# Weights in fp32 pieces on SyncE cast by GpSimd, a later gate for batch 2, and identity matmuls ahead of the first transposes

## Chip, cores, metric

One core of a Trainium2 chip. The metric is the device time of one execution in microseconds (us), median of several. "Ratio" is always the mean time of one kernel's fast runs over the mean of the fast runs of the kernel before of the same rounds, with a 95% interval; so it is not quite the ratio of the medians quoted beside it. Single executions of one kernel spread by 1 to 2 us.

Names: PE is TensorE, PEld its weight loads, DVE VectorE, ACT ScalarE, POOL GpSimd, SP SyncE. L824 is a line of the kernel; lines differ between versions. The granted clock is the share of its full speed that PE was given, by the profile. The milestone, below, is the start of the transposes of batch 1's first head group.

## The reference

```python
q_s = softmax(q, axis=-1); k_s = softmax(k, axis=2)        # 8 batches, 8 heads, 576 x 64
x = q_s @ (k_s^T @ v)                                      # heads put side by side: (8, 576, 512)
x_prev = x shifted by one position
xk = mu_k * x + (1 - mu_k) * x_prev
xr = mu_r * x + (1 - mu_r) * x_prev
k = relu(xk @ w_k)                                         # 512 -> 1024
out = sigmoid(xr @ w_r) * ((k * k) @ w_v)                  # 1024 -> 512
```

(Cut: the maxima and 1e-9 of the softmax, which the kernel leaves out.)

## The kernel before

A small planner in the kernel gives every piece of work an engine, an estimated length and a key, simulates the engines and emits each engine's instructions in the order that it finds. Each engine then runs its list in order, so the list decides what waits behind what. The parts that the argument touches (cuts marked):

```python
# weights: DMA with a cast, issued by GpSimd, after the eighth of batch 0's twelve loads
def emit_wk(g, c, e):
    ap = bass.AP(tensor=moe_w_k.tensor, ...)
    dst = wks[g][:, c * 2 // F, :, :] if split[g] else wks[g][:]          # bf16
    return nc.gpsimd.dma_start(out=dst, in_=ap)
# ... wr and wv likewise

# k = relu(...)^2: ScalarE evacuates, VectorE squares: two inputs, both in SBUF
def relu():
    nc.scalar.activation(out=rels[...], in_=bank(kf)[:, 0:n], func=ACT.Relu, scale=HALF_ROOT)
def square():
    nc.vector.tensor_tensor(out=k2s[...], in0=rels[...], in1=rels[...], op=ALU.mult)

# mu, transposed on PE into one of the four rotating banks (mm_a..mm_d), copied by VectorE
def emit_mu():
    nc.tensor.transpose(out=bank(mu_slot)[:, 0:8], in_=mu_sb[:], identity=identf[:])
def emit_mu_copy():
    nc.vector.tensor_copy(out=mu[:], in_=bank(mu_slot)[:, 0:8])
# ...
for op in plan.order():
    op.made = op.emit()
```

Batches 0 and 1 are prepared in the start: transposes of q and kv = k^T v of one head group ("transposes and kv": 72 small matmuls and as many weight loads, 0.66 us together at full speed), then "mixing" (products of 288 columns with mu folded in), then 32 k matmuls of 512 columns, then the transposes and kv of batch 1's first head group.

The softmax here doesn't subtract the row's maximum and nothing guards it: scores larger than these inputs give would overflow.

## Time and profile before

| | us |
|---|---|
| median of 3 runs | 201.63 (201.58 to 202.44) |
| first k matmul on record | 18.30 |
| PE at full speed from | about 22 |
| all 32 k matmuls done | 27.96 |
| transposes of batch 1's first group | 28.92, with 4 r matmuls done ahead of them |

Most lines behind this are in the prediction; the last is this one of the timeline of PE:

```profile
28.92 0.48 PE L507 MATMUL att_b<-ident,qs_a 64*64 64x64 bf16 x36
```

The trace has 2147 matmul records for 2171 weight loads, so some 24 matmuls are missing from it, among them the very first k matmul, here and in every trace of this study but those of the last three runs. Its weight load stands at 17.88 here, and the "0.34 <-issue" ahead of the first k matmul on record is no wait.

PE is full from 25 us to the end, so only the start has room.

### The profile page before, as it was taken

What the parts mean: (1) busy time and instruction counts of PE and PEld (TensorE: products, weight loads), DVE (VectorE), ACT (ScalarE), POOL (GpSimd) and SP (SyncE); (2) the same over time, 40 slices, a digit from 0 to 9 for tenths busy, and PEclk for the clock granted to TensorE, in tenths of its full rate; (3) what the DMA queues carried; (4) which work ended last, traced back from release to release, by engine and by line L of the source; (5) the groups of instructions that cost most, each with busy time, mean ns of one, the idle gap of its engine ahead of it and who ended that gap; (6) DMA issues with size and microseconds to landing.
All of it is one profiled execution on the core that took longest, in us unless ns stands there. A gap on an engine that the chain in (4) does not pass through costs nothing.

```text
span 200.2 us, 5314 instructions
## 1 busy us (share of the span) xinstructions
PE 183.6 (92%) x2147; PEld 96.6 (48%) x2171; DVE 160.6 (80%) x348; ACT 136.9 (68%) x212; POOL 40.7 (20%) x66
## 2 busy tenths in 40 slices
PE   2547999999999999999999999999999999999992
PEld 0234554545444555454476455455455544544761
DVE  2498469798999999999979999999998998432531
ACT  5494595998999799978559978946842662552440
POOL 1584365644354123411300000000000000000000
PEclk9999999999999999999999999999999999999998
DMA  6999999999999999993991220242042204402514
GB/s 196 348 277 227 281 256 352 391 398 412 388 403 405 403 405 362 398 378 110 262 365 47 54 56 0 52 111 51 3 100 62 52 3 105 105 0 54 118 41 105
DMA packets 15520, 40.72 MB, mean 203 GB/s; under 512 B 2300, under 2 KB 3592, under 8 KB 15496
## 3 DMA queue, kind: packets, MB, share of 16 engines
q0 software_dynamic: 7840, 27.40, 40.6%
q1 hardware_dynamic: 7208, 12.26, 21.4%
q10 hardware_dynamic: 448, 0.72, 1.2%
q8 instruction: 17, 0.28, 0.6%
q14 instruction: 7, 0.06, 0.1%
HBM read 33.56 MB, written 9.44 MB: 215 GB/s over the span
## 4 chain that ended last, share of the span: by engine, by line
PE 88%; DMA 4%; DVE 3%; issue 1%; ACT 1%; DVEq 0%
PE mm_c L766 10%; PE mm_a L722 10%; PE mm_d L722 9%; PE mm_d L766 8%; PE mm_a L766 7%; PE mm_c L722 7%; PE mm_b L766 6%; PE mm_b L722 6%; PE mm_b L756 6%; PE mm_d L756 4%; PE mm_c L756 3%; PE att_b L520 3%; PE mm_a L756 3%; DMA raw_d<-in_q_dram 3%; PE att_a L520 3%; PE att_b L507 2%
## 5 line engine op out<-in xcount | busy, mean ns | idle before, releaser
L722 PEld LDWEIGHTS <-wk 128*128 128x128 bf16 x320 | 35.4, 114 | 27.7 <-issue 2.2
L722 PE MATMUL mm_a<-xk,wk 128*128 128x512 bf16 (+1 forms) x96 | 24.2, 362 | 0.3 <-issue 0.2
L722 PE MATMUL mm_d<-xk,wk 128*128 128x512 bf16 (+1 forms) x87 | 22.4, 370 | 0.1
L766 PEld LDWEIGHTS <-k_b 128*128 128x128 bf16 x152 | 14.5, 98 | 15.7 <-issue 0.7
L756 PEld LDWEIGHTS <-xr 128*128 128x128 bf16 x144 | 13.9, 98 | 15.9
L766 PEld LDWEIGHTS <-k_a 128*128 128x128 bf16 x144 | 13.4, 97 | 15.5 <-issue 0.4
L722 PE MATMUL mm_c<-xk,wk 128*128 128x512 bf16 (+1 forms) x66 | 16.0, 358 | 0.4 <-issue 0.3
L722 PE MATMUL mm_b<-xk,wk 128*128 128x512 bf16 (+1 forms) x62 | 15.5, 352 | 0.2
L756 PE MATMUL mm_b<-wr_bf,xr 128*128 128x512 bf16 x50 | 13.3, 379 | 0.1
L766 PE MATMUL mm_c<-wv_bf,k_a 128*128 128x512 bf16 x46 | 12.1, 379 | 0.2 <-issue 0.2
L766 PE MATMUL mm_c<-wv_bf,k_b 128*128 128x512 bf16 x47 | 12.1, 379 | 0.2 <-issue 0.2
L761 ACT ACTIVATE th_a<-mm_b 128x512 f32<-128x512 f32 x12 | 7.1, 595 | 6.4 <-PE mm_b L756 4.9
L766 PE MATMUL mm_d<-wv_bf,k_b 128*128 128x512 bf16 x39 | 10.1, 379 | 0.2 <-issue 0.2
L766 PE MATMUL mm_b<-wv_bf,k_a 128*128 128x512 bf16 x38 | 10.0, 379 | 0.2 <-issue 0.2
L766 PE MATMUL mm_a<-wv_bf,k_b 128*128 128x512 bf16 (+1 forms) x39 | 9.4, 358 | 0.1
L756 PE MATMUL mm_d<-wr_bf,xr 128*128 128x512 bf16 x34 | 9.1, 379 | 0.1
L766 PE MATMUL mm_d<-wv_bf,k_a 128*128 128x512 bf16 x28 | 7.5, 379 | 0.4 <-issue 0.3
L710 DVE TENSOR_TENSOR k_a<-rel_b 128x512 bf16<-128x512 bf16 (+1 forms) x14 | 5.6, 398 | 2.8 <-ACT rel_b L706 2.8
L710 DVE TENSOR_TENSOR k_a<-rel_c 128x512 bf16<-128x512 bf16 (+1 forms) x13 | 5.1, 389 | 3.4 <-ACT rel_c L706 3.4
L761 ACT ACTIVATE th_b<-mm_c 128x512 f32<-128x512 f32 x6 | 3.7, 610 | 5.6 <-PE mm_c L756 4.7
L756 PE MATMUL mm_c<-wr_bf,xr 128*128 128x512 bf16 x28 | 7.2, 379 | 0.1
L756 PE MATMUL mm_a<-wr_bf,xr 128*128 128x512 bf16 x28 | 7.2, 379 | 0.0
(275 smaller groups left out, 416.7 us busy)
## 6 DMA issues: line engine op xcount, KB each, us to landing
out_dram<-ot_a SPq DMA_DIRECT2D x24, 128.0 KB, 3.8
out_dram<-ot_b SPq DMA_DIRECT2D x24, 128.0 KB, 3.0
out_dram<-ot_c SPq DMA_DIRECT2D x22, 128.0 KB, 2.8
raw_b<-in_k_dram POOLq DMA_DIRECT2D x3, 576.0 KB, 9.4
raw_c<-in_v_dram POOLq DMA_DIRECT2D x3, 576.0 KB, 8.9
raw_d<-in_q_dram POOLq DMA_DIRECT2D x3, 576.0 KB, 10.1
raw_a<-in_q_dram POOLq DMA_DIRECT2D x2, 576.0 KB, 10.5
raw_e<-in_k_dram POOLq DMA_DIRECT2D x2, 576.0 KB, 11.6
```

The costliest lines, as they stand in the source:

```text
L507: nc.tensor.transpose(out=transposed()[64 * u:64 * u + 64, hf, 64 * j:64 * j + 64], in_=qss[qs.index][r, j, 64 * u:64 * u + 64], identity= ...
L520: nc.tensor.matmul(bank(xp)[64 * hf:64 * hf + 64, u, at + c:at + e], lhsT=w[r, hf, :], rhs=qts[qt.index][r, hf, src:src + e - c], start=(n ...
L710: nc.vector.tensor_tensor(out=k2s[k2.index][:, fc, 0:n], in0=rels[rel.index][:, 0:n], in1=rels[rel.index][:, 0:n], op=ALU.mult)
L722: nc.tensor.matmul(bank(kf)[:, 0:n], lhsT=(w[:, h, u, fc % 4:F // 2:4] if split[ct // 2] else w[:, u, F // 2 * h + fc % 4:F // 2 * (h + 1) ...
L756: nc.tensor.matmul(bank(rps), lhsT=xs[1][:, ct, c:c + 128], rhs=wr_bf[:, ct // 2 + 2 * (ct % 2), :], start=(ct == 0), stop=(ct == CT - 1))
L761: nc.scalar.activation(out=ths[th.index][:], in_=bank(rps), func=ACT.Tanh, scale=0.5)
L766: nc.tensor.matmul(bank(vps)[:, 0:w], lhsT=k2s[k2.index][:, ft, 128 * m:128 * m + 128], rhs=wv_bf[:, ft, e:e + w], start=(ft == 0), stop=( ...
```

## The change

Its intent: weights come on the plain DMA queue in ten fp32 pieces of 512 KB, each early enough, and GpSimd, freed of issuing them, casts each into bf16. Batch 2's loads wait for the second half of batch 1's last q so that they do not take bandwidth from the start. Identity matmuls keep PE busy from 1.4 us, in the hope that its first k matmuls then run at full speed (in the kernel before PE was slow until about 22 us). The planner's offsets were tuned anew. Core of the diff:

```diff
-FIRST = ((0, 0, ("ACT", "ACT")), (0, 1, ("SP", "SP")), (0, 2, ("SP", "SP")), ...
+FIRST = ((0, 0, ("ACT", "ACT")), (1, 0, ("SP", "SP")), (0, 1, ("SP", "SP")), ...
-LOADS = ("q10a", "wk0a", "wk0b", "wk1", "k10a", ...
+LOADS = ("wk11", "k10a", "v10b", "wk01", "q10a", "q10b", "wr0", "k10b", "wk00", "wk10", ...
+W_CAST = ("POOL", "POOL", ... ten times)
-GATE = 7
-FILL = 0
+GATE = "q11b"
+FILL = 60
+    def load_weights(name, dst, offset, ap):
+        slot = Slot("raw")
+        ...
+        o = plan.add("SP", ..., lambda: nc.sync.dma_start(out=flat(), in_=...), [], [slot], ...)
+        return plan.add(e, ..., lambda: copies[e](out=dst[0], in_=flat()), [o], [], [slot])
     for _ in range(FILL):
+        plan.add("PE", 0.216, 0.386, 2 * LATE, lambda slot=slot: filler(slot), ...)
... (cut: NUDGE, 73 tuned offsets; EARLY, LOOK, SPARE, PACE; CASTS, now with all of batch 0's v on POOL; POOL's emit_wk, emit_wr, emit_wv removed)
```

Of the 60 identity matmuls (128x512) 18 find a place: 15 ahead of the first transposes, 3 later.

## The prediction

> **What bounds the kernel now.** I read the page first, then the busy times by stage, then PE's instructions in the start.
>
> The page: busy shares, PE by slices, DMA rate by slices (5 us each).
>
> ```profile
> PE 183.6 (92%) x2147; PEld 96.6 (48%) x2171; DVE 160.6 (80%) x348; ACT 136.9 (68%) x212; POOL 40.7 (20%) x66
> ...
> PE   2547999999999999999999999999999999999992
> ...
> GB/s 196 348 277 227 281 256 352 391 398 412 388 403 405 403 405 362 398 378 110 262 365 47 54 56 0 52 111 51 3 100 62 52 3 105 105 0 54 118 41 105
> ```
>
> PE is full from slice 5 to the last, so only the first 20 to 25 us can hold much. Busy times by stage (window, its length, then busy us and instructions of each engine):
>
> ```profile
> 8.00:18.30 10.30, 5.23 (x163) 3.94 (x153) 7.76 (x21) 7.03 (x11) 7.74 (x13) 1.00 1.05 271
> 18.30:24.50 6.20, 6.15 (x54) 2.88 (x55) 3.24 (x8) 2.60 (x6) 2.17 (x4) 1.00 1.12 279
> 24.50:44.40 19.90, 19.64 (x292) 9.88 (x295) 16.26 (x36) 16.96 (x30) 11.00 (x17) 1.00 1.04 350
> 44.40:196.00 151.60, 149.54 (x1616) 78.74 (x1633) 129.06 (x272) 105.67 (x164) 17.77 (x25) 1.00 0.54 177
> ```
>
> The second line looks full (6.15 of 6.20) and is not well used. The timeline of PE there (start, length, operation, shapes, count):
>
> ```profile
> 18.30 0.63 PE L722 MATMUL mm_c<-xk,wk 128*128 128x512 bf16 x1 [0.34 <-issue]
> ...
> 20.20 0.69 PE L520 MATMUL att_b<-qt_a,wp_b 64*64 64x288 bf16 x12
> ...
> 22.14 0.44 PE L520 MATMUL att_b<-qt_b,wp_d 64*64 64x288 bf16 x8
> 22.41 0.42 PE L520 MATMUL att_a<-qt_b,wp_d 64*64 64x288 bf16 x12
> ...
> 23.43 0.38 PE L722 MATMUL mm_d<-xk,wk 128*128 128x512 bf16 x1
> ```
>
> The same 12 products take 0.69 us at 20.2 and 0.42 at 22.4; a 512-column matmul 0.63 at 18.3 and 0.38 at 23.4. PE ran slow until about 22, though the granted-clock column says 1.00. And GpSimd, which issued the weights, held them back (waits of 8 to 31 us: total, times, longest):
>
> ```profile
> POOL raw_i L310 <- DMA wk<-in_moe_w_k_dram: 2.6, 1, 2.6
> POOL wv_bf L422 <- DMA wr_bf<-in_moe_w_r_dram: 2.0, 1, 2.0
> POOL raw_h L310 <- DMA wk<-in_moe_w_k_dram: 1.9, 1, 1.9
> ```
>
> The last wk wait ends at 21.99, and the first matmuls on wk's second half start at 22.76.
>
> **An account of PE.** Warm 512-column matmuls follow each other at 0.216 us (the chain shows 4 in 0.86). The network needs 288 for k, 144 for r, 288 for v: 720 x 0.216 = 155.4 us. Transposes and kv of one head group take 0.66 us (28.82 to 29.49 in the timeline), 16 times: 10.6. One mixing block of 20 products takes 0.72 with its changes of tile size, 8 times: 5.8. The other 12 x blocks take an estimated 0.3: 3.6. Together 175.4. The last matmul ends near 196.0, so about 20.5 us are lost, and 4.2 us follow. Before 18.3 PE does 2.8 us of this work (two pairs of transposes and kv, two mixing blocks): 15.5 lost. From 18.3 to 24.5 it does 4.9 (16 k matmuls, two blocks): 1.3 lost. From 44.4 to 196.0 it has 148.6 us of work left in 151.6: 3 lost in 150. The change lives in the first two terms.
>
> [...]
> - [...]0.69 against 0.42 us, changing near 22.0 after PE had been busy since 18.3.
> - [...]From 12 to 30 us 248 GB/s landed, 4.46 MB. I count 2.1 MB of it as bf16 weights that were read as 4.2 MB, so (4.46 + 2.1) / 18 = 364 GB/s were read, against 403 to 405 for plain loads in slices 12 to 15. The cast transfers thus cost nearly their fp32 bytes; fp32 pieces save about 10%, not half.
> - [...]the same 128x576 cast took 665 ns on POOL, 671 on ACT, 746 on DVE.
>
> **The change, part by part.**
> 1. *Weights.* Five cast transfers (512 or 256 KB of bf16) become ten fp32 ones of 512 KB on SyncE, each with a cast of 128x1024 on POOL: 665 x 1024/576 = an estimated 1.2 us, ten of them 12 us. [...]each piece needs 1.3 us of DMA at 404 GB/s, so POOL keeps up. But every piece has 1.2 us added before PE may use it.
> 2. *Order.* SyncE now issues wk11, k of batch 1 (half), wk01, q, wr0, k (half), wk00, wk10, wr1, v, four wv, then q, v, k of the second head group. Batch 0's 3.54 MB are down by about 12.1 (the last is used at 12.52 without a DMA wait). At 404 GB/s wk01 is complete after 1.34 MB more, 15.4; wk00 after 3.28, 20.2; wk10 after 3.80, 21.5; v after 4.91, 24.3; wv after 7.0, 29.5; the last k after 8.8, 33.8. [...]wk00 usable at 22.4, wk10 at 23.8.
> 3. *Identity matmuls.* Fifteen precede the first transposes: cold 0.43 each, some warm, so about 5 to 6 us from 1.4. They end before qs_a is complete (7.49) and delay nothing. With three more later, PE should stay warm through the start[...].
> 4. *Attention of batch 0.* The second q comes before k and v, so v lands at 9.5 to 10 instead of 8 to 8.6. POOL casts both v: two of 0.67, two mu_all pieces of 0.69, two of 0.67, and the second kv ends near 14.3 (before 14.7). In after's program all four mixing blocks come before the first k matmul. Walking their eight products (0.35 warm), evacuations (ACT 0.64, DVE 0.75) and the DVE weights (1.1 for four) through two att buffers, I get 18.4 for the first k matmul. Before had 18.3, with two blocks still to do.
> 5. *From there.* Sixteen warm k matmuls: 18.4 + 3.45 = 21.9. Wait for wk00 to 22.4, eight: 24.1; wk10 is there; eight more: 25.85, and the mu transpose, 26.0. Before finished all 32 at 27.96: 2.0 us gained.
> 6. *Given back.* Batch 1's v lands at 25.3 and ACT casts it in two of 0.67, so kv waits to 26.6: about 0.4 lost. wv is ahead of PE, which reaches v near 31. The second head group's k lands at 34.8, its exps end at 36.2, when PE gets there.
> 7. *After 44.* The same 150 us of work with a reordered list; 51 switches between small and full tiles against 49. I count nothing.
>
> Sum: -2.0 + 0.4, and -0.2 for the better-filled start of unit 1: about -1.8 us, 199.8.
>
> **Rivals.**
> - *POOL's casts become the bound.* If DVE and POOL hinder each other, a cast may take 1.8 us; ten are 18 and wv is late by some 3 us. For it: DVE is 76 to 82% busy in these stages. Against: POOL's 665 ns at 8 us, though DVE was idle then. It would make 201 to 202.5.
> - *PE goes cold again* between 8 and 18, as its waits there are long. The 16 k matmuls then cost up to 1.7 us more, half hidden in the wait for wk00: 200.8 to 201.5.
> - *The start is won in full*: mixing ends sooner and DMA lands without lag, and the retuned order takes 1 to 2 us of the 3 lost after 44. 197.3 to 198.5. For it: so many tuned offsets. Against: wk00's bytes cannot come before 20.2.
> - *Hidden anyway*: batch 2's loads, now gated on the second group's q (31 us), arrive late and PE waits near 50. DMA has the same bytes to move, so I give this little; 201.5.
>
> **Range and chances.** The main way gives 199.8, with 1 us either way from the lags and the cold clock; the rivals pull both ways. 197.9 to 201.4 holds it 8 times in 10. Over 2% faster means below 197.6: 9%. Over 2% slower needs a stall of 4 us: 2%.
>
> **What would show it.** Right: the 12-product blocks take 0.42 from their first; first wk matmul at 18 to 19; 32 k matmuls done by 26; casts of 128x1024 near 1.2 us; transfers of weights landing at 400 GB/s. Wrong: 0.69 blocks (cold), PE waiting over 1 us in total on POOL's wv casts, or PE's gaps after 44 us differing from 3 us by more than 1.

The sum above is -2.0 + 0.4 - 0.2, or about -1.8 us, 199.8. The allowance for a transfer's landing was read from no trace. It is in the times for wk00 (22.4, which is 20.2, the allowance and 1.2 for the cast), wk10 (23.8), v (25.3) and k (34.8), so the -2.0 and the 0.4 of parts 5 and 6 rest on it too. That busy time would keep PE at full speed (part 3) was the assumption, not shown by a trace, and so was the 1.8 us for a cast in the first rival; the longest whole cast measured took 1.63. The account's 0.72 and 0.3 us for a mixing and an x block are estimates; in the trace of the kernel before such blocks take 0.62 (42.01 to 42.63) and 0.37 (51.70 to 52.07) to the start of the next work.

## The result

The changed kernel took 204.35 us (203.87 to 204.44, 4 runs) against 201.97 (201.58 to 202.44, 4 runs): ratio 1.0112 [1.008, 1.0144]. It is 1.1% slower; 199.8 was predicted and 204.35 lies outside the range. The page of the changed kernel (busy shares, PE by slices, granted clock by slices, DMA rate by slices):

```profile
PE 188.9 (93%) x2165; PEld 98.8 (49%) x2189; DVE 161.9 (80%) x347; ACT 136.1 (67%) x211; POOL 42.6 (21%) x60
...
PEclk9965599999999999999999999999999999999999
...
GB/s 186 378 393 386 393 404 304 336 378 405 413 404 399 402 397 404 374 335 248 203 304 58 52 55 0 21 137 55 2 62 97 52 10 100 101 0 76 101 34 104
```

The transfers did what was hoped: 378 to 404 GB/s from 5 to 30 us instead of 227 to 348. The clock column now shows half speed from about 11 to 25 us. The busy times by stage, with the windows of the prediction (busy us of PE, PEld, DVE, ACT, POOL, then granted clock, DMA share, GB/s):

```profile
8.00:18.30 10.30, 7.20 (x189) 4.30 (x190) 8.59 (x24) 6.34 (x10) 6.95 (x10) 0.67 1.05 394
18.30:24.50 6.20, 5.22 (x47) 2.74 (x48) 4.40 (x8) 3.63 (x7) 3.00 (x4) 0.50 1.06 388
```

In 18.3 to 24.5, where 16 fast k matmuls were to run, the clock was 0.50 throughout.

I ran the same kernel once more (run again, below). It is a second execution to read. The first transposes:

```profile
9.84 0.48 PE L607 MATMUL att_a<-ident,qs_a 64*64 64x64 bf16 x36 [3.45 <-DVE qs_a L575]
```

```profile
7.92 0.48 PE L607 MATMUL att_a<-ident,qs_a 64*64 64x64 bf16 x36 [0.50 <-DVE qs_a L575]
```

The first line is of the first execution, the second of run again. The 3.45 us hole came from half of q landing late (VectorE stood 2.02 us behind it) in that one execution only; in the others of its kind, unless matmuls were added, the first transposes stand at 7.8 to 8.8. I read the start from run again.

The timeline of PE in run again (start, length, operation, and in brackets the idle time before with what ended it):

```profile
19.01 0.69 PE L620 MATMUL att_b<-qt_b,wp_d 64*64 64x288 bf16 x12 [0.45 <-DVE xk L678]
20.52 0.63 PE L824 MATMUL mm_a<-xk,wk 128*128 128x512 bf16 x1 [0.34 <-issue]
20.95 1.06 PE L824 MATMUL mm_b<-xk,wk 128*128 128x512 bf16 x2
...
24.10 0.59 PE L824 MATMUL mm_b<-xk,wk 128*128 128x512 bf16 x2
...
27.48 0.59 PE L824 MATMUL mm_a<-xk,wk 128*128 128x512 bf16 x2 [0.35 <-DVE mu L456]
...
29.73 0.48 PE L607 MATMUL att_a<-ident,qs_a 64*64 64x64 bf16 x36
```

Mixing products at 0.69 to 0.72, the first k matmul on record at 20.52 instead of 18.4 (the weight load of the missing first one is at 20.11), pairs of k matmuls at 1.06 and later at 0.59 (the listed lengths overlap; the starts are 0.85 and 0.43 apart): PE was slow until about 23.5. Then there is a wait for the copy of mu. The chain of waits of run again just ahead of it (start, length, what):

```profile
24.30 0.61 ACT rel_a L808
...
24.93 2.42 DVE k_a L812 x4
27.35 0.09 DVE mu L456
```

Four squares of 0.41 should take 1.65, not 2.42. VectorE and GpSimd there, from the timelines of run again:

```profile
25.43 1.25 DVE L812 TENSOR_TENSOR k_a<-rel_b 128x512 bf16<-128x512 bf16 x1
26.60 0.41 DVE L812 TENSOR_TENSOR k_a<-rel_c 128x512 bf16<-128x512 bf16 x1
...
27.27 0.15 DVE L456 COPY mu<-mm_a 128x8 f32<-128x8 f32 x1
```

```profile
25.18 1.23 POOL L501 CAST wr_bf<-raw_b 128x1024 bf16<-128x1024 f32 x1
```

The square beside the cast takes three times its length and ends 0.27 us after the cast does; the next, with GpSimd idle, takes 0.41. The mu copy sits behind them on VectorE, and its bank is the one that the k matmul at 27.48 needs.

A second loss lies near 78 us, in both executions of the changed kernel (first execution; timeline of PE):

```profile
76.83 1.24 PE L867 MATMUL mm_c<-wv_bf,k_a 128*128 128x512 bf16 x5
78.65 0.81 PE L867 MATMUL mm_c<-wv_bf,k_a 128*128 128x512 bf16 x3 [0.58 <-issue]
```

"Issue" means that PE waited for nothing that the profile shows. The kernel before has no issue gap over 0.3 us after the start.

To see where time goes I kept the prediction's account of PE: start time of a block, minus the full-speed work that PE has done by then. A matmul whose record is missing is counted by its weight load. What PE has lost, in us:

| lost by the block near | 29 us | 56 | 79 | 151 |
|---|---|---|---|---|
| before | 17.0 | 18.0 | 18.6 | 20.4 |
| changed (run again) | 18.6 | 19.4 | 21.0 | 22.1 |

The start loses 1.6 instead of gaining 2, 0.2 of it comes back by 56, about 1.0 more is lost around 79, and 0.7 is regained later. The retuned order may be what regains it; no run tests that.

### The profile page after: what moved, and what is told of

The parts are those of the page before. It is cut to its first block, busy times and chain, and to the rows that moved or that the text cites. A ratio compares the mean times of both kernels' runs of the same rounds, so it can differ in the third digit from the quotient of the medians.

```text
span 202.5 us, 5377 instructions
## 1 busy us (share of the span) xinstructions
PE 188.9 (93%) x2165; PEld 98.8 (49%) x2189; DVE 161.9 (80%) x347; ACT 136.1 (67%) x211; POOL 42.6 (21%) x60
## 4 chain that ended last, share of the span: by engine, by line
PE 82%; DVE 9%; DMA 3%; issue 3%; ACT 1%; ACTq 0%; DVEq 0%
PE mm_d L867 10%; PE mm_a L824 8%; PE mm_b L824 8%; PE mm_a L867 8%; PE mm_c L867 7%; PE mm_d L824 6%; PE mm_c L824 6%; PE mm_b L867 5%; PE mm_b L857 5%; PE mm_c L857 4%; PE mm_a L857 3%; PE att_b L620 3%; PE mm_d L857 3%; DMA raw_a<-in_q_dram 3%; PE att_a L620 2%
## 5 line engine op out<-in xcount | busy, mean ns | idle before, releaser
L824 PE MATMUL mm_a<-xk,wk 128*128 128x512 bf16 (+1 forms) x84 | 21.7, 366 | 0.5 <-issue 0.3
L824 PE MATMUL mm_b<-xk,wk 128*128 128x512 bf16 (+1 forms) x84 | 20.4, 360 | 0.0
L824 PE MATMUL mm_d<-xk,wk 128*128 128x512 bf16 (+1 forms) x74 | 19.1, 369 | 0.2 <-issue 0.2
L867 PE MATMUL mm_d<-wv_bf,k_b 128*128 128x512 bf16 (+1 forms) x71 | 15.9, 367 | 0.2 <-issue 0.2
L867 PE MATMUL mm_c<-wv_bf,k_b 128*128 128x512 bf16 x38 | 9.4, 379 | 0.3 <-issue 0.2
L867 PE MATMUL mm_a<-wv_bf,k_a 128*128 128x512 bf16 x38 | 9.5, 379 | 0.1
L867 PE MATMUL mm_c<-wv_bf,k_a 128*128 128x512 bf16 x32 | 7.9, 379 | 0.6 <-issue 0.6
L808 ACT ACTIVATE rel_a<-mm_a 128x512 bf16<-128x512 f32 x8 | 4.8, 602 | 4.6 <-PE mm_a L824 4.2
L867 PE MATMUL mm_a<-wv_bf,k_b 128*128 128x512 bf16 x31 | 7.5, 379 | 0.2 <-issue 0.2
L607 PE MATMUL att_a<-ident,qs_a 64*64 64x64 bf16 x288 | 3.9, 195 | 3.5 <-DVE qs_a L575 3.5
```

Of the source, the lines that this page charges most:

```text
L607: nc.tensor.transpose(out=transposed()[64 * u:64 * u + 64, hf, 64 * j:64 * j + 64], in_=qss[qs.index][r, j, 64 * u:64 * u + 64], identity= ...
L808: nc.scalar.activation(out=rels[rel.index][:, 0:n], in_=bank(kf)[:, 0:n], func=ACT.Relu, scale=HALF_ROOT)
L824: nc.tensor.matmul(bank(kf)[:, 0:n], lhsT=w[:, h, u, fc % 4:F // 2:4], rhs=xs[0][:, ct, c0:c0 + n], start=(ct == 0), stop=(ct == CT - 1))
L867: nc.tensor.matmul(bank(vps)[:, 0:w], lhsT=k2s[k2.index][:, ft, 128 * m:128 * m + 128], rhs=wv_bf[:, ft, e:e + w], start=(ft == 0), stop=( ...
```

## The experiments

Fifteen runs, each beside runs of the kernel before. From the second call on the expectations name their theories: A, the start is bound by VectorE, which the casts hold; C, it is bound by the slow clock; F, the hole near 78 us is PE waiting for its own instructions; G, the order of the loads makes it. A later run splits A into A1 (VectorE waits for a whole GpSimd instruction) and A2 (both share something at half rate).

### again: the changed kernel unchanged

> The changed kernel as it is, to see whether its late first transposes (second half of the first q used at 6.4 us, transposes at 9.8, PE clock 0.50 from about 11 to 25 us) come again. If they belong to the kernel: 204.3 us, transposes again at 9.5 to 10. If they were one execution's luck in the DMA: the half lands at 4.4 in this one, transposes near 7.5, time 201 to 202.

203.92 (203.66 to 204.08), ratio 1.01 [1.0068, 1.0132]. The late half of q did not come back; the time did not change. So the 3.45 us hole of the first execution cost nothing that can be told.

### no_ident: without the identity matmuls

```diff
 for op in plan.order():
+    if op.due >= 1.5 * LATE:
+        continue
     op.made = op.emit()
```

> The changed kernel with all 18 identity matmuls left out, the order of everything else untouched. Theory A (the second half of the first q comes late because of the loads beside it, and the identity matmuls end too early to help): transposes still near 9.8, PE slow till some 25 us all the same, 203.8 to 205. Rival B (the identity matmuls, or fetching their instructions, delay that load): the half lands near 4.4, transposes near 7.5, and the time falls to 202 or below. Rival C (the identity matmuls do help the clock somewhere): over 205.

203.14 (202.55 to 204.46), ratio 1.0068 [1.0022, 1.0113]: 0.8 us better by the medians, with intervals that overlap those of run again. The hole near 78 is gone. Here the k matmuls happened to run at full speed from the third, at 20.55. It brought nothing, for PE then waited (engine and what it waited for: total, times, longest):

```profile
PE mm_a L824 <- DVE mu L456: 1.5, 1, 1.5
PE mm_b L824 <- POOL wk L501: 0.8, 1, 0.8
```

and the milestone stands at 30.01 against 29.73 in run again. So theory C alone can't be the cause: fast or slow clock, the chain through VectorE ends at the same time.

### q2_from_k: the second half of batch 0's q read from k's tensor (wrong result)

```diff
-        src = (q, k, v)[i]
+        src = (q, k, v)[i] if (b, g, i) != (0, 1, 0) else k
```

> Wrong result on purpose: the q of the second head group of batch 0 is read from k's tensor (same shape, same place in SBUF, same queue and time), nothing else changed. If two loads from neighbouring rows of the same tensor hinder each other in HBM: the second half of the first q lands at about 4.4 as in the kernel before, transposes near 7.5, the PE hole is 1.3 us, and the time is 200.5 to 202. If only the traffic of the queues counts: lands at 6.3 again and 204.3 us.

204.3 (203.83 to 205.27), ratio 1.0123 [1.0084, 1.0161]. It was made to explain the late q half, which run again showed to be one execution's luck; it says nothing about tensors. Its trace is of use all the same: k matmuls at full speed from 19.68, the same 1.5 us wait for mu, 1.2 for the cast of wk00, milestone 29.73.

### more_ident: sixteen more identity matmuls ahead of the first transposes

```diff
+    more = 16
     for op in plan.order():
+        if more and op.engine == "PE" and op.due < 1.5 * LATE:
+            for i in range(more):
+                filler(SimpleNamespace(pool="mm", index=(i + 3) % 4))
+            more = 0
```

> The changed kernel with 16 more identity matmuls after the first 15 (16 x 0.216 = 3.5 us), so that PE has no hole before its first transposes at 9.8. Theory (the hole of 3.45 us let the clock fall, and the slow clock from 11 to 25 us costs about 1.8 us in the first k matmuls and up to 1 in the mixing blocks before): granted clock 1.00 throughout, first k matmul at 20.6 to 21.3 in place of 21.6, 32 k matmuls done 2 us earlier, 201.8 to 202.5. Rival (the wait for weights takes the place of the slow clock): PE waits at wk00 or wk10 and the gain is under 0.7 us.

207.12 (205.98 to 208.33), ratio 1.0257 [1.0199, 1.0315]: 3 us slower, yet its milestone is 29.91, nearly that of run again. The loss comes 45 us later (timeline of PE):

```profile
74.89 0.43 PE L584 MATMUL att_b<-vv_b,ek_b 64*64 64x65 bf16 x29
78.14 0.25 PE L584 MATMUL att_b<-vv_b,ek_b 64*64 64x65 bf16 x7 [2.82 <-issue]
```

A hole in the middle of 36 like matmuls has no data to wait for. The page shows an instruction queue (packets, MB, share):

```profile
q8 instruction: 17, 0.28, 0.6%
```

0.28 MB in 17 packets is 16 KB each. The changed kernel has 17 of them too, for 4,354 records of PE and its weight loads: one to 256, if all are PE's. Three of its packets began at 117.89, 129.07 and 140.62 us, and the view of windows counts 127 matmuls and 127 weight loads in the first stretch between them, 128 and 128 in the second. The packet of that place began at about 75.6 us and the hole ended at 78.14. Counting the records of PE and of its weight loads from the start, the matmul after the hole is number 1973 here and number 1972 in the changed kernel (a later expectation calls this place line 1978), where the added lines are fewer and the dense block ends 8 recorded matmuls ahead of it. In the nine holes of this kind that the kept traces hold, two of them in bef_rows below, such a packet began 2.3 to 2.6 us before the hole ended (76.27 and 78.65 in the changed kernel), and PE had gone through the 256 records ahead of the hole in 3.3 to 5.4 us (5.4 there; the median stretch of 256 records of that trace took 9.8). That PE waits for its own instructions there is theory F.

### mu_act: the mu copy on ScalarE

```diff
-        nc.vector.tensor_copy(out=mu[:], in_=bank(mu_slot)[:, 0:8])
+        nc.scalar.copy(out=mu[:], in_=bank(mu_slot)[:, 0:8])
```

> The changed kernel with the small copy of the transposed mu (128x8) on ScalarE instead of VectorE, nothing else. Theory A (the gain of the early k matmuls is taken back because the k matmul of the fifth use of the banks waits for this copy, which sits on VectorE behind squares that run beside GpSimd casts and take 1.25 us instead of 0.41): the wait of the k matmul for the mu copy (1.5 us in two runs so far, 0.35 in a third) is gone or below 0.3; the transposes and kv of batch 1 group 0 come 0.3 to 1.0 us earlier than 29.7 and the time is 0.3 to 1.0 us under the changed kernel's 204. Rival B (the copy is only one of several waits that end together; the squares still hold the rel products on ScalarE): the wait moves to the rel tiles, and the time stays within 0.3 us of 204. Rival C (the clock granted at the start is the cause): the time goes with the clock column and not with this wait.

203.88 (202.38 to 205.34), ratio 1.0091 [1.0027, 1.0156]: no gain, as rival B had it. The wait moved with the copy:

```profile
PE mm_d L824 <- ACT mu L456: 2.4, 1, 2.4
```

On ScalarE the copy stands behind the fourth relu, and that one waited 2.55 us for a free rel tile, that is for the held squares. The copy was the place where the delay showed, not its cause. The profiled execution was the slowest of the four: after this wait PE fell back to the slow clock (pairs of k matmuls at 1.06 from 28.0), and its milestone is 31.61. So this trace shows where the wait went, and not what the copy is worth.

### casts_act: three casts on ScalarE

```diff
-        ... lambda: copies[e](out=dst[0], in_=flat()), ...
+        ... lambda: copies["ACT" if name in ('wk00', 'wk10', 'wr1') else e](out=dst[0], in_=flat()), ...
```

> The changed kernel with three of the ten weight casts (wk00, wk10, wr1), those that run beside the squares of the first mixing, on ScalarE instead of GpSimd. Theory A: all squares between 22 and 27 us take 0.41 us instead of 1.25, no VectorE instruction there ends a quarter of a microsecond after a GpSimd cast any more, the mu copy is done before 26 instead of 27.3, the transposes and kv of batch 1 group 0 stand at 28.5 to 29.3 instead of 29.7 to 30.6, and the time is 0.5 to 1.5 us under 204. Rival B: the casts[...] push the rel products on ScalarE back by as much as VectorE gains, and the time stays within 0.4 us of 204. Rival C (clock): nothing moves except with the clock column.

204.29 (203.41 to 204.94), ratio 1.0109 [1.0063, 1.0156]. The step on the squares was right:

```profile
24.45 0.42 DVE L812 TENSOR_TENSOR k_a<-rel_a 128x512 bf16<-128x512 bf16 x1 [0.53 <-ACT rel_a L808]
24.94 0.42 DVE L812 TENSOR_TENSOR k_a<-rel_b 128x512 bf16<-128x512 bf16 x1
```

and the step to the time was wrong. The cast of wk00 now stood between the second and third relu on ScalarE for 0.94 us, PE waited 0.7 for it, PE was slow until 23.3, the mu copy was done at 27.36, hardly earlier than in run again (27.4), and the milestone came at 29.7. The hole near 78 was there too (0.8). The three casts were listed with 1.05 to 1.07 us each on ScalarE. Rival B was right of this version.

### combo: no identity matmuls, mu copy and the same three casts on ScalarE

> All three together: no identity matmuls at the start, mu copy on ScalarE, three casts on ScalarE. Theory A adds the parts: 0.8 us from leaving out the identity matmuls (measured: 203.1 against 203.9 to 204.3), up to 1.5 us from the squares and the copy: 201.5 to 202.5 us, as fast as the kernel before or a little faster. If the squares are not the cause: 203 or more.

201.91 (201.82 to 203.41), ratio 0.9991 [0.9951, 1.0031]: as fast as the kernel before, as theory A had it, but not by its sum. Of the three parts two had brought nothing alone. Its milestone is 30.3, late, and it has no hole near 78. I don't read more from it.

### two_casts: no identity matmuls, casts of wk10 and wr1 on ScalarE

> The candidate: the changed kernel without identity matmuls, with only the casts of wk10 and wr1 on ScalarE; wk00 stays on GpSimd (it ended at 22.8, before its use), the mu copy stays on VectorE. Theory A: squares of the first mixing take 0.41 us, the mu copy is done by 25.5 to 26.5, no k matmul waits over 0.4 us for the mu copy or for a weight cast; where TensorE is warm at 20.5 the transposes of batch 1 group 0 stand at 27.5 to 28.5, where it is cold until 23.5 at 29 to 29.5; time 200.5 to 202.0, ratio 0.993 to 1.001 against the kernel before. If something else held the start (rel evacuations, the vv copies on ScalarE): 202 or more, and the wait list names it.

201.56 (201.26 to 202.83), ratio 0.9982 [0.9949, 1.0015]. It differs from no_ident in two casts alone, those beside the squares, and is 1.6 us below it by the medians (0.9% by the ratios, whose intervals do not overlap). It was run at another time. Squares 0.41, mu copy done at 26.3, no k matmul waits for it, milestone 28.64 with a slow clock until 22.3 (timelines of VectorE and of PE):

```profile
25.37 0.41 DVE L812 TENSOR_TENSOR k_a<-rel_c 128x512 bf16<-128x512 bf16 x1
```

```profile
28.64 0.48 PE L607 MATMUL att_a<-ident,qs_a 64*64 64x64 bf16 x36
```

This is the clearest single test of A in time.

### pieces: every GpSimd cast cut into four

```diff
-        ... lambda: copies[e](out=dst[0], in_=flat()), ...
+        def cast():                       # cut: casts not on POOL stay whole
+            for r in range(2):
+                for c in range(0, 512, 256):
+                    copies[eng](out=dst[0][:, r, c:c + 256], in_=flat()[:, r, c:c + 256])
```

> The changed kernel with every GpSimd weight cast (128x1024) cut into four of 128x256, nothing else. Theory A1 (a VectorE instruction that starts beside a GpSimd cast waits until that one instruction ends): each piece takes about 0.3 us, so a square beside a cast takes at most 0.7 us instead of 1.25, the mu copy comes about 1 us earlier, and the time is 0 to 1 us under the changed kernel's 204 (the hole near 78 us and the slow clock at the start stay). Rival A2 (the two engines share something at half rate all through a cast): squares beside casts still take over 1 us, and the casts 1.2 us and more for four pieces; the time stays at 204 or rises.

202.89 (202.03 to 203.22), ratio 1.0028 [0.9978, 1.0077]. The work is the same and on the same engine, only the instructions are shorter (timeline of VectorE, then of GpSimd):

```profile
24.12 0.53 DVE L821 TENSOR_TENSOR k_a<-rel_a 128x512 bf16<-128x512 bf16 x1
24.60 0.57 DVE L821 TENSOR_TENSOR k_a<-rel_b 128x512 bf16<-128x512 bf16 x1
...
25.63 0.61 DVE L821 TENSOR_TENSOR k_a<-rel_a 128x512 bf16<-128x512 bf16 x1
```

```profile
23.03 2.41 POOL L506 CAST wk<-raw_l 128x256 bf16<-128x256 f32 x4 [0.65 <-DMA raw_l<-in_moe_w_k_dram]
```

All four squares ran beside casts and none took over 0.61: A1, and not A2. The casts pay: four pieces alone take 1.44 instead of 1.04, and 2.41 beside VectorE. The mu copy is done 1.1 us earlier (26.17 against 27.27 in run again), the milestone stands at 28.89, and the time is 1.0 to 1.5 us under the changed kernel's two medians. The hole near 78 (0.8) is still there.

### two_casts_pieces: the last two together

> The candidate of the last call (no identity matmuls, casts of wk10 and wr1 on ScalarE; 201.56 us there) with the remaining GpSimd casts in four pieces each. Theory A1: the squares at 29 to 33 us, 1.23 and 0.79 beside the casts of wv, come under 0.7, TensorE loses less between 28.6 and 39.8 us (1.7 us there), and the time is 0.3 to 1.2 us under 201.6: 200.4 to 201.3, ratio 0.991 to 0.998 against the kernel before. Rival A2: 201.6 or more.

201.96 (201.17 to 203.14), ratio 0.9997 [0.9957, 1.0036]. The squares at 29 to 33 us came to 0.48 to 0.64, and the account of its profiled execution is lower (20.2 lost by the block near 151 against 21.2 in two_casts), but the medians don't show it; the expectation of 200.4 to 201.3 missed.

### bef_rows and bef_rows3: the kernel before with more lines of program

```diff
+    tiny = 32                                   # bef_rows3: 96
     for op in plan.order():
+        if tiny and op.engine == "PE":
+            for i in range(tiny):
+                nc.tensor.matmul(ps["mm"][3][:][:, 0:32], lhsT=ident[:], rhs=ident[:, 0:32],
+                                 start=True, stop=True)
+            tiny = 0
```

> The kernel before, with 32 tiny identity matmuls (128x32, [...]in the time when TensorE has no other work) ahead of its first work: only the number of TensorE instructions ahead of everything changes, by 64 lines of its program. Theory F (instructions reach TensorE in packets of 256, and where a packet's boundary falls in two dense blocks of transposes and kv near 75 us, TensorE runs out of them; the kernel before had its boundary elsewhere by luck): a hole marked issue of 0.5 to 3 us between 72 and 80 us that the kernel before does not have, and 0.5 to 3 us more time (202.5 to 205). Rival G (the hole comes with the changed order of the loads): no hole, time within 0.3 us of the kernel before.

205.11 (203.93 to 206.03), ratio 1.015 [1.0094, 1.0206]. 32 matmuls that took 1.03 us, in time when PE had nothing to do, cost 3.3 us. The milestone was even earlier (28.4). Then two holes (timeline of PE):

```profile
76.40 0.29 PE L484 MATMUL att_a<-vv_b,ek_b 64*64 64x65 bf16 x13 [1.37 <-issue]
...
108.56 0.23 PE L484 MATMUL att_b<-vv_a,ek_a 64*64 64x65 bf16 x5 [1.25 <-issue]
...
109.23 1.06 PE L722 MATMUL mm_b<-xk,wk 128*128 128x256 bf16 x4
```

The matmul after the first is number 1972 again, at the place of more_ident, and that after the second is number 2737, 765 further, which is three packets of 256 records to within the few that a trace misses. After the second PE ran at half speed for some 3 us: the four matmuls of 256 columns at 109.23 take 1.06, where they take 0.60 in the kernel before.

> The kernel before with 96 of the tiny identity matmuls ahead of its first work instead of 32: three times the added work, but 192 more lines of program instead of 64. Theory F (packets of 256 instructions: the runs so far put boundaries at line 1978 plus or minus multiples of 256; a hole comes where two boundaries are crossed within some 4 us, as happens in two dense blocks of transposes and kv that follow each other): with 192 lines no two boundaries fall into one such pair, so the holes of the run with 64 lines (1.4 us at 75 and 1.25 us at 107) are gone and the time is within 0.6 us of the kernel before, 201.3 to 202.5. Rival G (any more work of TensorE at the start costs time later, whatever its number of lines): 205 or more, more than with 32.

202.61 (202.46 to 203.21), ratio 1.0036 [1.0001, 1.0072]: three times the added work, no issue hole over 0.3 us, and 0.5 us instead of 3.3. So it isn't the work at the start but the place of the lines, and rival G falls: the kernel before has the order of its own loads and shows the holes.

### wv_pieces, warm_fill, warm_fill5: is the slow clock the rest?

All three: no identity matmuls at the start, casts of wk10 and wr1 on ScalarE, those of wv in pieces. The second and third have identity matmuls in the holes of the mixing stage:

```diff
+    fill = {(0, 1, 0): 2, (0, 1, 1): 1}         # warm_fill5: 3 and 2
     for op in plan.order():
+        ...                                      # cut: identity matmuls of the start left out
+        for _ in range(fill.pop(getattr(op, "tag", None), 0)):
+            filler(SimpleNamespace(pool="mm", index=0))
         op.made = op.emit()
```

> Control for the next two: no identity matmuls, casts of wk10 and wr1 on ScalarE, only the four casts of wv cut into four pieces each (wk00 whole, as in pieces its cast took 2.4 us and TensorE waited 0.3 for it). Expected by both theories: 201.2 to 202.0, transposes of batch 1 group 0 at 28.3 to 29.7 where TensorE is cold until 22.3 to 23.4.

202.09 (201.58 to 203.47), ratio 0.9999 [0.996, 1.0037]; milestone 28.16.

> The control with three identity matmuls in the holes of the mixing stage (two ahead of the third mixing block, one ahead of the fourth, holes of 0.74 and 0.45 us)[...]. Theory W (what is still missing from the predicted gain, once GpSimd's casts no longer hold VectorE, is the slow clock of the first seven k matmuls, 0.43 instead of 0.22 us each, 1.5 us): k matmuls take 0.22 from the first or second, the transposes of batch 1 group 0 stand at 27 to 27.8, and the time is 0.5 to 1.5 us under the control. Rival V (a further wait of VectorE or ScalarE takes its place, or the clock does not answer to this): the same time as the control within 0.3 us, or more by the time of the added matmuls.

201.91 (201.0 to 202.72), ratio 0.9979 [0.9943, 1.0015]. The timeline of PE has the fast clock from within the mixing stage (its last products take 0.42):

```profile
15.96 1.04 PE L483 MATMUL mm_a<-ident 128*128 128x512 bf16 x2
...
19.17 0.62 PE L834 MATMUL mm_a<-xk,wk 128*128 128x512 bf16 x2
...
24.90 0.59 PE L834 MATMUL mm_d<-xk,wk 128*128 128x512 bf16 x2 [0.57 <-ACT rel_a L818]
...
27.68 0.48 PE L616 MATMUL att_a<-ident,qs_a 64*64 64x64 bf16 x36
```

The first k matmul is at 19.17 (19.66 in the control), the milestone at 27.68, the earliest of all fifteen runs, with new waits of 0.3 for wk00 and 0.57 for a relu. In the time, 0.2 us by the medians, it can't be told from its control.

> As the run before with five identity matmuls (three and two). Theory W: warm from the first k matmul, but up to 0.8 us later; time 0.3 to 1.2 us under the control. Rival V: 0.3 to 0.9 us over the control.

202.23 (201.12 to 203.02), ratio 0.9994 [0.9959, 1.0029]. Fast clock again, from 17.3, but PE then waited 1.3 us for the cast of wk00, and the milestone is 28.77.

So the fast clock can be had, and what it gains is mostly taken by the next wait. Theory W is right on the clock and not shown in the time.

## Why the prediction was wrong, point by point

Three steps failed. In part 3 PE was to stay warm; it fell back to the slow clock. The sum of parts 1, 5 and 6 gave each cast a time on GpSimd and none on VectorE; squares beside casts took up to 1.25 us instead of 0.41. And part 7 had no term for the place of PE's instructions; the hole near 78 us took 0.58 and 0.70 us in the changed kernel's two executions. The first two lie over each other in the start, as point 5 shows.

1. *Weights.* A cast of 128x1024 took 1.04 us alone (1.2 estimated), and up to 1.63 beside VectorE. The estimate of the cast was fine. What failed is what the step left out: what a cast does to VectorE.
2. *Order and DMA.* wk00 was usable at 22.80 (22.4 predicted) in run again, wk10 at 25.2 (23.8), the latter because its cast was held too (1.44). Right within 0.4 us where GpSimd was not held.
3. *Identity matmuls.* "PE should stay warm through the start" failed. It was fast from 4.7 us in the first execution and slow again from 11 (from 6.8 to 10.4 in run again), after a start at 1.36 in both. The prediction had named this as a rival at 200.8 to 201.5. How much busy time the fast clock needs is not shown by these runs; k matmuls turned fast anywhere from 19 to 25 us in runs of like kernels. The granted-clock column was no sure sign of it: it showed 1.00 in no_ident while mixing products took 0.69. The lengths of like instructions were surer.
4. *First k matmul at 18.4.* 20.11 by its weight load (20.52 is the second). The walk used 0.35 us for a mixing product at full speed; they took 0.69 to 0.72. The clock's share in these 1.7 us is known only in part: fillers in the mixing stage brought the first k matmul from 19.66 to 19.17 (wv_pieces, warm_fill), and in q2_from_k, fast from 17.4, its weight load stands at 19.44. That is 0.5 to 0.7 us. No run was fast through the whole stage, so the rest stays open. The 18.3 that the prediction read for the kernel before is the second k matmul too; the first is at 17.88.
5. *32 k matmuls done by 26.0.* 29.73, 3.7 late. In run again: 1.7 from the late start; 1.4 from the first sixteen, which took 5.38 us (20.11 to 25.49) instead of 3.45 and the 0.55 us of waiting for wk00 that was allowed; 0.6 from the second sixteen, 4.08 instead of 3.45, with the 0.35 us wait for mu. That is the sum of one execution. The other limit is hidden behind it: with the clock fast (no_ident, q2_from_k) the waits for mu and wk00 take its place, and the milestone is still 29.7 to 30.0. Two limits of about equal length lay over each other, so taking away one (mu_act, casts_act, fast clock by luck) showed nothing; pieces, which gave no other engine new work, is the exception.
6. *Given back, 0.4, by late v.* In run again kv of batch 1 follows its transposes at once, at 30.03, so v cost nothing there. What gave the gain back was VectorE: the squares beside the casts are the missing term. The rival on POOL saw the pair of engines but looked for the harm on the casts ("wv is late by some 3 us"); it was on VectorE's squares.
7. *Nothing after 44 us.* Right in the sum, for two unlike terms: about 1.0 lost around 79 us, mostly to the hole, and 0.7 regained. The prediction had no step for the number of PE's instructions.

Which of VectorE's instructions a cast holds can be read from the trace of the changed kernel. Two kinds with two inputs in SBUF took longer beside one: squares (0.89 us instead of 0.41 at 26.14, 0.66 at 30.00; both end 0.27 us after the cast does, as the one of 1.25 in run again) and qs (1.35, without a cast 0.75). With one input, the reduction of eq kept its 0.70 (at 22.99, beside the cast at 22.65), and the copy of xk out of PSUM its 0.76 (at 16.25, beside the cast at 15.81). I had named the rival and not gone through VectorE's instructions one by one.

The sum of the loss by pairs of runs: again to no_ident 0.8 us (with the hole), no_ident to two_casts 1.6 us; together 2.4, against 2.0 to 2.4 lost. The first term alone is not resolved in time; that the hole goes with the identity matmuls is: all seven runs with the eighteen (after, again, q2_from_k, more_ident, mu_act, casts_act, pieces) have a hole of 0.5 us or more there, and none of the seven without (no_ident, combo, two_casts, two_casts_pieces, wv_pieces, warm_fill, warm_fill5) has. Left open: why the corrected versions, with a start up to 1.2 us earlier than the kernel before in the profile, are not clearly faster than it. They have done four r matmuls (0.86 us) fewer at the milestone, which takes most of it; the rest is within the spread. No version beat the kernel before by more than its interval.

## What to carry to other kernels

Before moving work to GpSimd, list VectorE's instructions with two SBUF inputs in that stage. Here a square beside a whole cast of 128x1024 took up to 1.25 us instead of 0.41, and the four squares of the start 0.53 to 0.61 beside casts in four pieces; so try short pieces (their price here: a cast took 1.44 instead of 1.04 alone, and 2.41 beside VectorE), or give the casts to ScalarE. When one removal shows nothing, look for a second limit that ends at the same time, and take away both. And count instructions: here 32 matmuls of 1.03 us in all, on an idle PE, cost 3.3 us of time and 96 cost 0.5, which theory F puts down to where the boundaries of the packets fell among dense runs of short matmuls.
